# A scan feeding a mixture of experts: first tiles gathered a tile ahead, the padding row written later, and one conditional block put inside the other

## The chip, the cores and the metric

The kernel runs on one core of a Trainium2 chip. The metric is the device time of one execution in microseconds, as the median of several runs. One further execution is profiled, and all rows of a trace below come from that one.

## The reference

The input is a sequence of 4 x 5056 = 20224 tokens with 256 channels. A gated recurrence runs over the tokens of each of the four sequences, and its output is the input of a mixture of eight experts, of which each token uses one:

```
f = lower_bound + (1 - lower_bound) * sigmoid(f_logit)
h[t] = f[t] * h[t-1] + (1 - f[t]) * x[t]          # per sequence and channel
logits = h @ w_gate                               # 8 experts
e = argmax(logits); gate = softmax(logits)[e]; eom = sigmoid(h @ w_output_gate)[e]
out = gate * eom * (relu(h @ w1[e]) @ w2[e])      # w1: 256 x 1024, w2: 1024 x 256
```

## The kernel before

The kernel has two kinds of work that run interleaved.

**Chunks.** The tokens come in 40 chunks of 512 (`chunk`). For each chunk the SP queue loads the gate logits and the inputs, channels on the partitions (`load_chunk`, L250 and L251, two buffers each). ScalarE takes the tanh (L265), VectorE and ScalarE form the terms, VectorE runs the scan (L280). The result is scaled and split into a high and a low half in 16 bits (L310, L314), both halves lie in the buffer of the gate logits, and SP turns them into rows with DMA transposes (L307, four per chunk, into the tile `rows`). TensorE computes the router's logits (L329), VectorE picks the expert and the token's place among that expert's tokens, and POOL scatters each row, with a factor and the token's number behind it, to that place in a DRAM scratch `scr` (L433, an indirect DMA for each 128 tokens). A chunk is a generator that is cut into 17 steps; one "pump" advances every live chunk by one step, and a new chunk begins every eight pumps once the first ones are under way. In its fifth step a chunk asks for the next chunk's loads. The next but one chunk's loads use the same buffers, so they wait until the transposes have read them.

**Tiles.** A tile is a group of rows of one expert that is read back from `scr` by `gather`: SP reads the tile's address from a table that VectorE has filled (`plan_first`, `plan`), then issues a DMA transpose of the rows into `xq` (L630, three buffers) and a small load of their factors and token numbers into `mt` (L633, four buffers). Both wait for the scatters that the plan covers. The tile's factor `fac` on VectorE multiplies the factor in `mt` with a constant of the expert (L649). After two matrix products ScalarE scales the result by `fac` (L746), and POOL writes the rows to the output at the token numbers that it reads from `mt` (L750, an indirect DMA). An `mt` buffer is free again when that write is done.

The 16 *first tiles* (two rounds of one 128-row tile for each expert) run while the expert weights are still being loaded and split: `prep_load` loads half an expert's matrix in two pieces (L566), and other helpers scale and split it. Their work is cut by half tile. The loop over `j` from -2 to 15 (one half expert matrix each) calls `early` twice per `j`, then a drain loop calls it until all first tiles are through. Each call may gather one tile into `line`, takes the oldest tile of `line` one half further (`first1`, L715 to L717), makes the low half of the half before (`first_low`, L726), runs the second product of the half before that (`first2`, L735 to L737), and writes out finished tiles. A tile of expert `e` can be gathered when `j` is at least 2e+1 and computed from `j` = 2e+2. Between the calls `step` runs a number of pumps.

After that come the *later tiles*: 64 of 256 rows and a tail of up to 37 of 128 rows (`experts`). Each takes its expert's first matrix in a copy (L657), the products are L669 to L671 and L702 to L704. How many of the tail's 37 are used depends on the tokens. 18 of them are always run; the next 3 and the last 16 stand in two conditional blocks, one after the other, each behind a test of the count that every engine makes for itself (L964, L966). With these inputs neither block runs. Where a block is skipped, each engine brings the semaphores up to the values that the block would have left.

The order of the instructions: each engine works through its own queue in order. SP's queue follows the program's order. In the part up to the end of the first tiles (`prog["cut"]`) the scheduler of the framework may reorder the instructions of the four compute engines; behind that the order is as written. The first entries of SP's queue are a write of zero rows that stand for padding (`padt`, L211; POOL fills the tile, L209 and L210), then the loads of chunks 0 to 2 and the first weight pieces.

Of the kernel before, what the change touches and what calls it, by code (L numbers as in the profile page):

```python
# [45 lines left out]
def raw(ins):  # L46
    return getattr(ins, "ins", ins)
# [3 lines left out]
def tile_scan_moe(  # L51
# [10 lines left out]
    nc = tc.nc  # L62
    P = 128
# [10 lines left out]
    FREE = E * R  # L74
# [9 lines left out]
    def sure(tokens):  # L84

        return max(0, -(-(tokens - len(EARLY) * E * P - E * 255) // 256))
# [8 lines left out]
    scr = dp.tile([E * R + P, RW], I16, name="scr")  # L95
# [8 lines left out]
        out=tri, in_=ones, compare_op=ALU.is_gt, fill=0.0, base=0, pattern=[[1, P]], channel_multiplier=-1  # L104
# [63 lines left out]
    def alone(g):  # L168
# [12 lines left out]
        out=gsq, in0=wgf, scalar=1.0, in1=wgf, op0=ALU.mult, op1=ALU.mult, accum_out=gss  # L181
# [9 lines left out]
        out=wgs[:, :, 1, :], in0=wgc, scalar=gsc, in1=wgs[:, :, 0, :], op0=ALU.mult, op1=ALU.subtract  # L191
# [3 lines left out]
    fresh = []  # L195

    def apart(ins, group, keep=()):
        tc.declare_no_dep(raw(ins), group=group, keep=[raw(k) for k in keep], reason="rows apart")
        tc.add_to_no_dep_group(group, raw(ins))
# [8 lines left out]
    padt = cp.tile([P, RW], I16, name="padt")  # L208
    nc.gpsimd.memset(padt, 0)  # L209
    nc.gpsimd.iota(padt[:, CM + 2 : CM + 4].bitcast(I32), pattern=[[0, 1]], base=N, channel_multiplier=0)  # L210
    fresh.append(nc.sync.dma_start(out=scr[FREE : FREE + P, :], in_=padt))  # L211
    apart(fresh[0], "scr")
    row2 = [cp.tile([P, NB, RW], I16, name=f"rows{i}") for i in range(2)]

    top1 = w1f[:, (E - 1) * 2 * WH : E * 2 * WH]
# [344 lines left out]
    half = {}  # L560

    def prep_load(j):
        ws = []
        for i in range(2):
            w = wp.tile([P, QH], F32, tag="w", name="w")
            nc.sync.dma_start(out=w, in_=wT[j // 2][:, j % 2 * WH + i * QH : j % 2 * WH + (i + 1) * QH])  # L566
            ws.append(w)
        half[j] = dict(w=ws)
# [47 lines left out]
    def prep_lo(j, z):  # L616
        (h, r), (l, _) = parts(j, 0, z), parts(j, 1, z)
        yield BIG
        nc.vector.scalar_tensor_tensor(out=l, in0=r, scalar=half[j]["sc"], in1=h, op0=ALU.mult, op1=ALU.subtract)
# [4 lines left out]
    def gather(t, slot, e=None):  # L624
        tab, j, nb, new = slot
        n = nb * P
        r = nc.sync.value_load(tab[j : j + 1, 0:1], min_val=0, max_val=FREE + P - n)
        xq = gp.tile([P, 2, KD, 256], I16, tag="xq", name="xq")
        mt = gp.tile([P, 2, 4], I16, tag="mt", name="mt", bufs=4)
        i1 = nc.sync.dma_start_transpose(  # L630
            out=xq.rearrange("p a k n -> p (a k) n")[:, :, 0:n], in_=scr[ds(r, n), 0 : 2 * D]
        )
        i2 = nc.sync.dma_start(out=mt[:, 0:nb, :], in_=scr[ds(r, n), CM : CM + 4].rearrange("(b p) d -> p b d", p=P))  # L633
        for ins in (i1, i2):
            for k in new:
                tc.add_manual_dep(raw(ins), raw(k).name, DATA, reason="rows scattered")
            apart(ins, "scr", new)
        return dict(xh=xq[:, 0].bitcast(F16), xl=xq[:, 1].bitcast(F16), mt=mt, nb=nb, tab=tab, j=j, id=t, ev=e)
# [83 lines left out]
    def first_low(T, h):  # L722
        ph, hh = T[f"h{h}"]
        hl = ep.tile([P, 4, P], F16, tag="el", name="el", bufs=3)
        yield BIG
        nc.vector.scalar_tensor_tensor(out=hl, in0=ph, scalar=0.0, in1=hh, op0=ALU.max, op1=ALU.subtract)  # L726
        T[f"h{h}"] = (hh, hl)
# [31 lines left out]
    total = sure(N)  # L759
# [68 lines left out]
    line, pend, mid, over = [], [], [], []  # L828
    turns = [0] * len(EARLY)

    def early(j):

        if not line or line[0]["half"] == 1 and len(line) == 1:
            for r in range(len(firsts)):
                e = turns[r]
                if e < min(E, (j + 1) // 2) and (r == 0 or e < turns[r - 1]):
                    T = gather(f"f{r * E + e}", firsts[r][e], e)
                    T["half"] = 0
                    line.append(T)
                    turns[r] += 1  # L840
                    break
        tasks, wait, ready, late = [], list(pend), list(over), list(mid)
        pend.clear()
        over.clear()
        mid.clear()
        for T, h in wait:
            tasks.append(first_low(T, h))
            if h == 0:
                tasks.append(factors(T))
        go = line and line[0]["ev"] < j // 2  # L850

        def rest():
            for T in ready:
                evacuate(T)
                put(T)
            if go:
                T, h = line[0], line[0]["half"]
                T["half"] += 1
                if h == 1:
                    line.pop(0)  # L860
                first1(T, h)
                pend.append((T, h))
            for T, h in late:
                first2(T, h)
                if h == 1:
                    over.append(T)
            mid.extend(wait)

        return tasks, rest
# [6 lines left out]
            prep_load(n - 1)  # L876
    for n in range(min(EARLY[0], NCH) - 1, deep):
        prep_load(n)
    for j in range(-2, nh):
        tasks = []  # L880
        if 1 <= j < nh + 1 - deep:
            prep_load(j - 1 + deep)
        if 0 <= j + 1 < nh:
            tasks.append(prep_scale(j + 1))
        for z in range(2):
            if 0 <= j:
                tasks.append(prep_lo(j, z))
            mine, rest = early(j)
            tasks += mine
            step((PUMPS if j >= TURN else PUMPS0 if j >= 0 else FILL) / 2, tasks, LEAD)  # L890
            if 0 <= j + 1 < nh:
                prep_hi(j + 1, z)
            rest()
            tasks = []
            if j + 2 < nh:
                if z == 0:
                    prep_gram(j + 2)
                    tasks.append(prep_norm(j + 2))
                else:
                    prep_sum(j + 2)  # L900
# [10 lines left out]
    def ordered(start, cut):  # L911

        loose = [e.engine for e in (nc.vector, nc.scalar, nc.tensor, nc.gpsimd)]
        prev = {}
        for i, ins in enumerate(nc.cur_bb.bb.instructions[start:]):
            free = i < cut and ins.engine in loose
            if ins.engine in prev and not free:
                tc.add_manual_dep(ins, prev[ins.engine], AFTER, reason="order")
            prev[ins.engine] = ins.name

    def experts(t0, t1, more):
        ahead(t0)
        alone(expert(tiles[t0]))
        alone(fetch1(tiles[t0], 0))
        for t in range(t0, t1 + 2):
            T = tiles.get(t) if t < t1 else None
            U = tiles.get(t - 1) if t0 < t <= t1 else None
            V = tiles.get(t - 2) if t > t0 + 1 else None
            rate = RATE * (T or U or V)["nb"] / 2
            for q in range(4):  # L930
                tasks = []
                if q == 0:
                    if t + 1 < t1 + min(more, 1):
                        ahead(t + 1)
                    if T:
                        tasks.append(fetch1(T, 1))
                elif q == 2:
                    if t + 1 < t1:
                        alone(expert(tiles[t + 1]))
                        tasks.append(fetch1(tiles[t + 1], 0))  # L940
                elif q == 3 and T:
                    tasks.append(factors(T))
                if q == 0 and U:
                    tasks.append(low(U, 3))
                if q and T:
                    tasks.append(low(T, q - 1))
                step(rate, tasks)
                if q == 0 and V:
                    evacuate(V)
                if q == 1 and V:  # L950
                    put(V)
                if T:
                    gemm1(T, q)
                if U:
                    gemm2(U, q)

    cuts = [n for n in MORE if n < tail] + [tail]
    between["on"] = True
    experts(0, total + cuts[0], len(cuts) - 1)
    beside()  # L960
    ordered(0, prog["cut"])

    if len(cuts) > 1:
        used = nc.values_load(prog["count"][0:1, 0:1], min_val=0, max_val=tail)  # L964
        for a, b in zip(cuts[:-1], cuts[1:]):
            with tc.If(used > a):  # L966
                experts(total + a, total + b, 0)
                ordered(0, 0)


# [36 lines left out]
```

## Time and profile before

| what | us |
|---|---|
| runs | 986.54, 992.43, 989.42 |
| median of the runs | 989.42 |
| the profiled execution | 990.77 |
| its span, first to last instruction | 989.1 |
| TensorE busy, matmuls | 907.7 (92%) |
| VectorE busy | 801.0 (81%) |
| ScalarE busy | 519.7 (53%) |
| POOL busy | 390.1 (39%) |

The mean granted TensorE clock was 0.988. The busy times are averages over stages of different kinds, so they are read by stretches of the span. A wait in the profile names the instruction that waits and the one whose end released it. In a row of the timeline the first number is the start in microseconds, the second the duration, the bracket the idle time of the engine just before it and what ended that. Rows of SP with the letter q are instructions of its DMA queue.

### The profile page before, as it was taken

To read this page: it belongs to the slowest core of one execution; us is meant where nothing else is said; L and a number is where in the kernel's file an instruction comes from. 1 tells how busy PE (TensorE), PEld (TensorE's weight loads), DVE (VectorE), ACT (ScalarE), POOL (GpSimd) and SP (SyncE) were. 2 spreads that over 40 slices of the span, in tenths; PEclk is the share of its full clock that TensorE was granted. 3 is DMA by queue.
4 is the path that set the end of the run, shared out by engine and by line. 5 is a ranking of instruction groups with operands and counts; after the bars stand their busy time and mean duration, and the time that the engine had idled before them with its cause. 6 is when DMAs were issued, how large, how long until landed. Compare 5 with 4: busy or idle time off the path is not lost. (4 is left out here: it accounts for less than half of the span.)

```text
span 989.1 us, 30907 instructions
## 1 busy us (share of the span) xinstructions
PE 907.7 (92%) x9775; PEld 819.7 (83%) x9775; DVE 801.0 (81%) x2639; ACT 519.7 (53%) x1075; POOL 390.1 (39%) x378
## 2 busy tenths in 40 slices
PE   2258898899999999999999999999999999999993
PEld 2247887788888888888888888888888888899992
DVE  7989897888989988888898888888888886545550
ACT  6667675555555555555565555555555543333331
POOL 1432334434445454454545434455444443211111
PEclk9999999999999999999999999999999999999997
DMA  8899984855575657556576665655666544312120
GB/s 310 206 275 293 237 230 126 188 157 151 131 157 144 151 153 167 141 133 152 150 153 150 169 138 140 153 148 157 150 163 134 129 100 90 100 45 43 41 57 17
DMA packets 238558, 146.56 MB, mean 148 GB/s; under 512 B 202557, under 2 KB 204223, under 8 KB 238400
## 3 DMA queue, kind: packets, MB, share of 16 engines
q1 hardware_dynamic: 222752, 101.74, 44.9%
q0 software_dynamic: 15360, 42.74, 14.4%
q8 instruction: 95, 1.56, 0.7%
q14 instruction: 63, 0.52, 0.2%
q10 hardware_dynamic: 288, 0.02, 0.0%
HBM read 58.38 MB, written 44.49 MB: 104 GB/s over the span
## 5 line engine op out<-in xcount | busy, mean ns | idle before, releaser
L674 ACT ACTIVATE hh<-ph 128x512 f16<-128x512 f32 (+1 forms) x328 | 180.4, 550 | 307.8 <-PE ph L671 297.4
L669 PE MATMUL ph<-xq,w 128*128 128x256 f16 (+1 forms) x1312 | 330.4, 260 | 2.9 <-DMA xq<-scr 2.4
L671 PE MATMUL ph<-xq,w 128*128 128x256 f16 (+1 forms) x1312 | 331.1, 261 | 0.0
L670 PE MATMUL ph<-xq,w 128*128 128x256 f16 (+1 forms) x1312 | 330.9, 261 | 0.0
L750 POOL DMA_INDIRECT out_dram<-yo,mt x146 | 175.3, 1201 | 363.2 <-ACT yo L746 339.9
L704 PE MATMUL py<-w2s,hl 128*128 x1168 | 318.5, 273 | 0.0
L703 PE MATMUL py<-w2s,hh 128*128 x1168 | 318.4, 273 | 0.0
L702 PE MATMUL py<-w2s,hh 128*128 x1168 | 318.1, 272 | 0.0
L682 DVE SCALAR_TENSOR_TENSOR hl<-ph,hh 128x512 f16<-128x512 f32 (+1 forms) x328 | 204.9, 625 | 58.2 <-ACT hh L674 55.8
L433 POOL DMA_INDIRECT scr<-rows,dst x154 | 175.7, 1141 | 122.6 <-issue 109.3
L657 DVE COPY w<-w1s 128x2048 f16 x164 | 120.3, 734 | 35.1 <-PE ph L671 33.3
L669 PEld LDWEIGHTS <-w 128*128 128x128 f16 x1312 | 127.9, 98 | 14.3 <-DVE fac L649 2.7
L671 PEld LDWEIGHTS <-w 128*128 128x128 f16 x1312 | 128.0, 98 | 11.9
L670 PEld LDWEIGHTS <-w 128*128 128x128 f16 x1312 | 127.9, 97 | 9.7
L704 PEld LDWEIGHTS <-hl 128*128 128x128 f16 x1168 | 114.1, 98 | 13.8
L702 PEld LDWEIGHTS <-hh 128*128 128x128 f16 x1168 | 114.0, 98 | 11.4
L703 PEld LDWEIGHTS <-hh 128*128 128x128 f16 x1168 | 113.9, 98 | 10.6
L280 DVE TENSOR_TENSOR_SCAN xt<-ft,xt 128x512 f32<-128x512 f32 (+4 forms) x78 | 90.8, 1172 | 0.0
L746 ACT ACTIVATE yo<-py,fac 128x256 f32<-128x256 f32 x146 | 61.8, 468 | 26.7 <-PE py L704 26.1
L314 DVE SCALAR_TENSOR_TENSOR ft<-xt,sa,ft 128x512 f16<-128x512 f32 (+1 forms) x76 | 56.2, 744 | 20.1 <-ACT ft L265 18.3
L329 PEld LDWEIGHTS <-ft 128*128 128x128 f16 x600 | 51.7, 99 | 15.1 <-ACT ft L310 4.9
L310 ACT ACTIVATE ft<-xt,sa 128x512 f16<-128x512 f32 (+1 forms) x76 | 50.2, 707 | 23.3 <-DVE li L299 16.0
(171 smaller groups left out, 1298.7 us busy)
## 6 DMA issues: line engine op xcount, KB each, us to landing
ft<-in_fT_dram SPq DMA_DIRECT2D x37, 512.0 KB
xt<-in_xT_dram SPq DMA_DIRECT2D x37, 512.0 KB
w<-in_wT_dram SPq DMA_DIRECT2D x32, 512.0 KB
scr<-rows,dst POOLq DMA_INDIRECT x154
rows<-ft SPq DMA_TRANSPOSE x152
out_dram<-yo,mt POOLq DMA_INDIRECT x146
xq<-scr SPq DMA_TRANSPOSE x99
scr<-padt SPq DMA_DIRECT2D x9, 136.0 KB
```

The lines of the kernel that those rows point to most:

```text
L280: nc.vector.tensor_tensor_scan(out=xt[:, k, a:z], data0=ft[:, k, a:z], data1=xt[:, k, a:z], initial=init, op0=ALU.mult, op1=ALU.add)
L433: ins = nc.gpsimd.indirect_dma_start(out=scr[:, :], out_offset=IOA(ap=dst[:, b : b + 1], axis=0), in_=rows[:, b, :], in_offset=None)
L657: nc.vector.tensor_copy(out=w, in_=w1f[:, ds(T["ev"] * (2 * WH) + h * 2 * QH, 2 * QH)])
L669: nc.tensor.matmul(out=o, lhsT=w[:, f, k, 0, :], rhs=T["xh"][:, k, 0:n], start=first, stop=False)
L670: nc.tensor.matmul(out=o, lhsT=w[:, f, k, 0, :], rhs=T["xl"][:, k, 0:n], start=False, stop=False)
L671: nc.tensor.matmul(out=o, lhsT=w[:, f, k, 1, :], rhs=T["xh"][:, k, 0:n], start=False, stop=last)
L674: nc.scalar.activation(hh[:, :, 0:n], ph[:, :, 0:n], AF.Relu)
L682: nc.vector.scalar_tensor_tensor(out=hl[:, :, 0:n], in0=ph[:, :, 0:n], scalar=0.0, in1=hh[:, :, 0:n], op0=ALU.max, op1=ALU.subtract)
L702: nc.tensor.matmul(out=o, lhsT=hh[:, i, c], rhs=wh, start=first, stop=False, skip_group_check=True)
L703: nc.tensor.matmul(out=o, lhsT=hh[:, i, c], rhs=wl, start=False, stop=False, skip_group_check=True)
L704: nc.tensor.matmul(out=o, lhsT=hl[:, i, c], rhs=wh, start=False, stop=last, skip_group_check=True)
L750: ins = nc.gpsimd.indirect_dma_start(out=out[:, :], out_offset=IOA(ap=T["mt"][:, b, 2:4].bitcast(I32), axis=0), in_=T["yo"][:, b, :], in_o ...
```

## The change

Four edits. The write of the padding rows moves behind the loads of the prologue. `early` gathers a tile whenever fewer than two are in line. The factors of a first tile are made in the call after its second half, no longer in the call after its first. And the second conditional block stands inside the first, so that one test is made where the first block is skipped; with it the first later tile of a block is gathered inside the block.

```diff
     padt = cp.tile([P, RW], I16, name="padt")
     nc.gpsimd.memset(padt, 0)
     nc.gpsimd.iota(padt[:, CM + 2 : CM + 4].bitcast(I32), pattern=[[0, 1]], base=N, channel_multiplier=0)
-    fresh.append(nc.sync.dma_start(out=scr[FREE : FREE + P, :], in_=padt))
-    apart(fresh[0], "scr")
...
     def early(j):
 
-        if not line or line[0]["half"] == 1 and len(line) == 1:
+        if len(line) < 2:
             for r in range(len(firsts)):
...
         for T, h in wait:
             tasks.append(first_low(T, h))
-            if h == 0:
+            if h == 1:
                 tasks.append(factors(T))
...
     for n in range(min(EARLY[0], NCH) - 1, deep):
         prep_load(n)
+    fresh.append(nc.sync.dma_start(out=scr[FREE : FREE + P, :], in_=padt))
+    apart(fresh[0], "scr")
     for j in range(-2, nh):
...
-    experts(0, total + cuts[0], len(cuts) - 1)
+    experts(0, total + cuts[0], 0)
     beside()
     ordered(0, prog["cut"])
 
+    def rest_of(i):
+        if i + 1 < len(cuts):
+            with tc.If(used > cuts[i]):
+                experts(total + cuts[i], total + cuts[i + 1], 0)
+                ordered(0, 0)
+                rest_of(i + 1)
+
     if len(cuts) > 1:
         used = nc.values_load(prog["count"][0:1, 0:1], min_val=0, max_val=tail)
-        for a, b in zip(cuts[:-1], cuts[1:]):
-            with tc.If(used > a):
-                experts(total + a, total + b, 0)
-                ordered(0, 0)
+        rest_of(0)
```

## The prediction

> **What bounds the kernel now.** I read the page first, then the stretches table, the waits, and the timeline of the stretches that the change touches. The stretches table, cut at the points where the 16 first tiles end and where the last matmul ends (columns: busy time of PE, PEld, DVE, ACT, POOL, then granted clock, DMA share, GB/s):
>
> ```profile
> 0.00:184.00 184.00, 121.93 (x1652) 111.45 (x1652) 154.87 (x548) 119.32 (x216) 60.07 (x78) 0.98 0.89 235
> 184.00:973.00 789.00, 785.80 (x8124) 708.24 (x8123) 646.08 (x2092) 400.14 (x859) 329.07 (x299) 1.00 0.55 131
> 973.00:989.10 16.10, 0.00 (x0) 0.00 (x0) 0.00 (x0) 0.28 (x1) 0.98 (x1) 0.56 0.04 7
> ```
>
> There are three stages. In the middle one TensorE is busy 785.8 of 789.0 us, its matmuls and their order are not touched by the diff, so nothing is to be had there. The change can act on the first 184 us, where no engine is full (DVE 84%, PE 66%, DMA share 0.89) and the time is set by waits, and on the 16 us after the last matmul. Of the first stage's waits two belong to the gathers of first tiles, the weight side of TensorE left out:
>
> ```profile
> PE ph L715 <- DMA xq<-scr: 12.8, 6, 3.7
> DVE fac L649 <- DMA mt<-scr: 8.5, 7, 3.8
> ```
>
> (total us, times, longest.) Not all of the 12.8 us can be reached, as the call order below shows.
>
> **Part 1: the padding row written later.** The start, from the timeline and the SP queue's own waits:
>
> ```profile
> SPq L211 <- POOL rows L398: 2.7, 1, 2.7
> 0.83 0.38 ACTq L122 DMA_DIRECT2D lbt<-in_lbT_dram  x1
> ...
> 3.16 0.38 SPq L211 DMA_DIRECT2D scr<-padt  x1
> ...
> 3.60 0.42 SPq L250 DMA_DIRECT2D w2s<-in_fT_dram  x1
> ...
> 5.13 0.25 DVE L190 SCALAR_TENSOR_TENSOR wgs<-wgc,gts,wgs 128x32 f16<-128x32 f32 x1
> ...
> 7.65 1.15 ACT L265 ACTIVATE w2s<-w2s 128x512 f32<-128x512 f32 x2 [4.65 <-DMA w2s<-in_fT_dram]
> ...
> 9.04 1.29 DVE L269 SCALAR_TENSOR_TENSOR w2s<-w2s 128x512 f32<-128x512 f32 x2 [3.66 <-DMA w2s<-in_xT_dram]
> ```
>
> The first instruction of SP's queue is the padding write, which waits 2.7 us for POOL to fill its tile, and the first load stands behind it at 3.60. Without it that load can go when ACT's first one went, at 0.83: 2.8 us earlier, with all loads of the prologue behind it. ACT waits 4.65 and DVE 3.66 us for exactly these two loads, and DVE's own preparations end at 5.4, before the 6.3 that its next step would move to. So nothing else takes the wait's place and the shift is whole: 2.8 us. The write itself (0.38 us of SP) moves behind the last early weight load, where SP then waits for ACT anyway: nothing. Bounds: 2.3, if DVE's preparations or the shared start of the queues cost half a microsecond, and 3.2, if the write had also held the engines of the DMA.
>
> **Part 2: first tiles a tile ahead.** One call of `early` is one half tile. Before, tile n+1 is gathered in the call of tile n's second half; now in the call of its first half, where the expert's bound allows it. Following the loops with their counts of pumps (6 per half of j before j=0, then 1.5, then 1.125), the first four gathers stay where they are: rounds and experts are not ready sooner. From the fifth on each moves up by one call, but on SP's queue only five pass anything: the fifth passes the two loads of chunk 7, the seventh the first two row transposes of chunk 6, the eighth the other two, the fourteenth the first two of chunk 8, the fifteenth the other two. The rest stand in the same place of the queue as before.
>
> Now the middle of the stage:
>
> ```profile
> 92.81 0.38 SPq L250 DMA_DIRECT2D ft<-in_fT_dram  x1
> ...
> 99.12 1.15 ACT L265 ACTIVATE ft<-ft 128x512 f32<-128x512 f32 x2 [1.19 <-DMA ft<-in_fT_dram]
> 100.91 1.13 POOL L750 DMA_INDIRECT out_dram<-ey,mt  x1 [14.27 <-ACT ey L746]
> 101.01 0.23 PE L715 MATMUL ph<-xq,w1s 128*128 128x128 f16 x1 [2.00 <-DMA xq<-scr]
> 101.27 2.59 SPq L307 DMA_TRANSPOSE rows<-ft  x2
> 104.90 1.74 SPq L630 DMA_TRANSPOSE xq<-scr  x1
> 109.08 0.38 SPq L633 DMA_DIRECT2D mt<-scr  x1
> ...
> 113.01 2.59 SPq L307 DMA_TRANSPOSE rows<-ft  x2
> ...
> 119.45 0.38 SPq L250 DMA_DIRECT2D ft<-in_fT_dram  x1
> ...
> 121.78 0.22 PE L715 MATMUL ph<-xq,w1s 128*128 128x128 f16 x1 [1.05 <-DMA xq<-scr]
> 123.98 1.15 ACT L265 ACTIVATE ft<-ft 128x512 f32<-128x512 f32 x2 [3.57 <-DMA ft<-in_fT_dram]
> ```
>
> The fifth tile (PE idle 2.00 before 101.01) and the eighth (1.05 before 121.78) get their data sooner: 3.1 us of PE's waits. With the factors moved one call back, DVE loses all 8.5 us of its waits for `mt`, of which 3.8 lie at the fourteenth tile (below) and 4.7 here. Against that stands what is queued behind. A gather takes about 2.0 us of SP (161.89 to 163.88 below), so chunk 7's load goes 2.0 later than 92.81, and ACT, which already waited 1.19 for it, waits 3.2. The seventh gather is worse: `mt` has four buffers, so its load may only go when the third tile's output write (issued 100.91) has landed. In this trace SP stood at that point until 109.08. Passing the transposes of 101.27, SP reaches it at about 103.5 (the 2.0 us of a gather after 101.3) and stands there 5.6 us with the transposes behind it: they go at 109.5 instead of 101.3, those of 113.01 at about 115.5, behind the eighth gather, and the load of 119.45, which follows their landing, at about 122, 2.5 late. ACT waited 3.57 for that load. So gains of up to 4.7 on DVE face losses of up to 2.0 + 2.5 = 4.5 on ACT. I take a gain of 1.0, since DVE is the fuller engine; ends: +4.7 and -4.5.
>
> The Trainium skill, "DMA: Bandwidth & Descriptors" (section "Anatomy of one DMA"), speaks against the change here: it says that a DMA's semaphore fires only when its last byte is confirmed as landed, and that waits on semaphores are made by the issuing sequencer before dispatch, so an early gather holds its whole queue; the 8.2 us from 100.91 to 109.08 agree. By its fit of about 2.0 us plus bytes over 436 GB/s that write would, as an estimate, land near 103, and the hold would nearly vanish; the row decides.
>
> The end of the stage:
>
> ```profile
> 158.05 2.99 SPq L307 DMA_TRANSPOSE rows<-ft  x2
> 161.60 0.18 DVE L369 TENSOR_REDUCE km<-key 128x4 f32<-128x32 f32 x1
> 161.89 1.24 SPq L630 DMA_TRANSPOSE xq<-scr  x1
> ...
> 163.88 2.52 SPq L307 DMA_TRANSPOSE rows<-ft  x2
> 164.74 0.23 PE L715 MATMUL ph<-xq,w1s 128*128 128x128 f16 x1 [3.26 <-DMA xq<-scr]
> 165.58 0.21 DVE L649 TENSOR_SCALAR fac<-mt,cinv 128x1 f32<-128x1 f32 x1 [3.79 <-DMA mt<-scr]
> ...
> 171.72 0.96 POOL L433 DMA_INDIRECT scr<-rows,dst  x1 [5.67 <-DVE pl_av L497]
> ...
> 178.69 1.26 SPq L630 DMA_TRANSPOSE xq<-scr  x1
> ...
> 184.55 0.28 PE L669 MATMUL ph<-xq,w 128*128 128x256 f16 x1 [0.47 <-DVE w L657]
> ```
>
> The fourteenth gather stands behind transposes that wait for chunk 8's lower halves (158.05). PE idles 3.26 us for its rows and DVE 3.79 for its `mt`, and behind DVE's stall hang chunk 8's positions, its scatter at 171.72, and the gather of the first later tile at 178.69. Passing those transposes, it goes while SP is idle. PE runs nearly without gaps from 164.74 to 184.55, so its end moves by up to 3.26. What is late next: the transposes at 163.88 do not go sooner, because the fifteenth gather now stands ahead of them, and their landing bounds the scatter. I take 2.5 of the 3.26; ends 0 and 3.8.
>
> **Part 3: the second block inside the first.** Neither block runs here (82 later tiles, no more). The unused gather of tile 82 goes; SP waits for nothing behind it: 0. The rows of both skipped blocks and of the closing:
>
> ```profile
> 973.55 0.98 POOL L750 DMA_INDIRECT out_dram<-yo,mt  x1 [2.08 <-ACTq L966]
> L966 PEldq COMPARE_BRANCH  x2: 3852/4162/4472, 972.9 to 977.1; - x2
> L966 POOLq COMPARE_BRANCH  x2: 45/45/45, 973.9 to 976.5; - x2
> L966 POOLq INC_SWDGE_SEM  x2: 2322/2328/2335, 974.2 to 977.0; - x2
> L1003 POOLq DRAIN  x3: 40/107/8885, 979.4 to 988.8; - x3
> L1003 PEldq DRAIN  x2: 8/8/8, 981.9 to 988.7; - x2
> ```
>
> PE's second branch costs 4.47 us, but PE is through at 981.9. POOL ends the program: two skips, each a branch and a 2.33 us semaphore step (974.2 and 977.0), then a drain of 8.9 us from 979.4 to 988.3. One skip less starts the drain up to 2.86 us sooner (977.0 less 974.2). But the one step that is left accounts for writes on all queues' semaphores, so it must wait for the last write, issued 973.55 to 974.53 and by the rows landed before 977.0; I put it at 976.0, which leaves 1.0 us. What holds the drain for 8.9 us no row says: if it is tied to the last write, 0 comes; if to the two steps, 1.0 + 8.9/2, about 5.4.
>
> By the Trainium skill, "Runtime: NRT & Kernel Launch" (section "Instruction fetch mechanics"), a taken branch out of the fetched window stalls for a fetch; PE's 3.85 and 4.47 us agree. If the end hung on PE, 4.8 would come instead of 1.0.
>
> **Sum.** 2.8 + 1.0 + 2.5 + 1.0 = 7.3 us. The profiled execution took 990.77 us (span 989.1 and 1.7 around it): 983.5. It lies 1.35 above the median of the runs, 989.42, so the median forecast is 982.1 us.
>
> **Rivals.**
> (a) The gain at the fourteenth tile is swallowed: the fifteenth gather delays the transposes, the scatter stays near 171.7 and the gather of 178.69 with it. For: the queue's order; against: the scatter follows DVE's late positions. 989.4 - 4.8 = 984.6.
> (b) The closing drain depends on the skipped steps, or the end hangs on PE's branch: 989.4 - 7.3 - 4.4 = 977.7. For: two steps, one long drain; against: PE ends 6 us before POOL.
> (c) Slower: SP's hold at the seventh gather goes through whole. The price is 5.6 plus 2.0 for chunk 7's load, and no gain in this stage: 989.4 - 2.8 - 1.0 + 7.6 = 993.2. It decides once chunk 8's load goes more than 3.8 us later, counted from the first load, than now. For: ACT waits for loads at 99 and 124; against: SP catches up behind the weight loads.
> (d) The first load does not go at 0.83 because something else holds SP: 984.9. Against: the only wait in its rows is the one for POOL.
>
> **How the numbers follow.** Forecast 0.50 (979 to 985.5, from the bounds of the parts without their extremes together), (a) 0.17, (b) 0.15, (c) 0.08, (d) 0.05, and 0.05 for an order of the engines' work in the first stage that the scheduler, free there, changes for the worse by some 5 us. Leaving out most of (c) and the far end of (b), the range is 976.5 to 988. Half a per cent, about what this kernel's runs can tell from no change, is 4.9 us: faster means below 984.5. Faster: 0.46 of the forecast's, 0.15 of (b), 0.08 of (a) and 0.02 of (d), 0.71. Slower, above 994.4: 0.04. Same: 0.25.
>
> **What would show it.** Right: the first load near 0.8 and ACT's first activation near 4.9; no wait of `fac` for `mt`; PE not idle at the fourteenth tile; the first matmul of a later tile about 6 us earlier, near 178; TensorE's middle stage as long as before; POOL's drain starting about 1 us closer to the last write. Wrong: SP's wait at the seventh `mt` with longer ACT waits at chunks 7 and 8; the start of later tiles still above 181; a drain shorter or longer than 8.9 us.

## The result and the profile after

The changed kernel takes 1003.75 us (median; 1000.63 to 1005.82), the kernel before, run beside it, 988.89. The ratio is 1.0145 with a 95% interval of 1.0104 to 1.0185: 14.9 us slower, where the prediction had 7.3 us faster. The profiled execution took 1005.82 us, its span is 1004.0.

The stretches of the changed kernel, cut just before the first matmul of a later tile and after the last matmul (columns as in the prediction):

```profile
0.00:200.70 200.70, 123.05 (x1652) 111.28 (x1653) 157.16 (x556) 119.72 (x219) 63.86 (x80) 0.89 0.81 215
200.70:988.70 788.00, 787.01 (x8123) 708.75 (x8122) 641.22 (x2083) 399.58 (x856) 326.84 (x297) 1.00 0.56 131
```

The middle stage is what it was (788.0 us, 789.0 before, TensorE full). The whole loss lies in the first stage, which ends near 201 instead of 184.5. TensorE and VectorE are busy for about as long as before in it (123 and 157 us); they wait more. Its start went as predicted (rows of the timeline; after the change, lines behind the old place of the padding write stand two lower):

```profile
0.82 0.46 SPq L248 DMA_DIRECT2D w2s<-in_fT_dram  x1
4.59 1.15 ACT L263 ACTIVATE w2s<-w2s 128x512 f32<-128x512 f32 x2 [1.55 <-DMA w2s<-in_fT_dram]
6.25 1.29 DVE L267 SCALAR_TENSOR_TENSOR w2s<-w2s 128x512 f32<-128x512 f32 x2 [2.11 <-DMA w2s<-in_xT_dram]
```

The first load goes at 0.82 (3.60 before), ScalarE starts at 4.59 (7.65) and VectorE's scan work at 6.25 (9.04): 2.8 to 3.1 us. By chunk 6's load (70.92, before 70.06) that lead is gone, and at the end of the stage there is a lag of 16.6. Here the seventh gather with what follows it, and the way to the first later tile:

```profile
105.39 1.22 SPq L628 DMA_TRANSPOSE xq<-scr  x1
...
111.20 0.37 SPq L631 DMA_DIRECT2D mt<-scr  x1
111.67 3.69 SPq L305 DMA_TRANSPOSE rows<-ft  x2
...
145.56 0.96 POOL L431 DMA_INDIRECT scr<-rows,dst  x1 [2.16 <-issue]
...
190.67 0.97 POOL L431 DMA_INDIRECT scr<-rows,dst  x1 [5.62 <-issue]
...
196.96 1.26 SPq L628 DMA_TRANSPOSE xq<-scr  x1
...
201.17 0.37 PE L667 MATMUL ph<-xq,w 128*128 128x256 f16 x1 [5.80 <-DMA xq<-scr]
```

Read it from the bottom. The first later tile starts at 201.17, 5.80 us after TensorE ran dry, because its gather went at 196.96 (178.69 before). The gather follows the scatter of chunk 8, at 190.67 (171.72 before). Chunk 6's scatter goes at 145.56; before it went at 132.84. So 12.7 of the 19 us were lost by chunk 6's scatter, nearly all of them behind its load, which goes 0.9 late; the lead of 2.8 was used up ahead of it. The waits of the first stage (total us, times, longest), after and then two of the kernel before that were not shown:

```profile
DVE fac L647 <- DMA mt<-scr: 19.6, 8, 4.2
ACT ft L263 <- DMA ft<-in_fT_dram: 17.9, 4, 7.6
SPq L631 <- DMA out_dram<-ey,mt: 15.3, 4, 6.3
```

```profile
SPq L633 <- DMA out_dram<-ey,mt: 4.4, 2, 2.2
ACT ft L265 <- DMA ft<-in_fT_dram: 8.0, 5, 3.6
```

VectorE's waits for `mt` did not vanish, they grew from 8.5 to 19.6 us, and ScalarE's for the loads of the gate logits from 8.0 to 17.9. SP stands four times, 15.3 us, at the load of `mt` until an output write has landed. At the other end of the program:

```profile
989.11 0.98 POOL L748 DMA_INDIRECT out_dram<-yo,mt  x1 [2.06 <-ACT yo L744]
L965 POOLq EVENT_SEMAPHORE  x4: 17/43/43, 989.6 to 991.9; - x4
L965 POOLq INC_SWDGE_SEM  x1: 2342/2342/2342, 992.0 to 992.0; - x1
L1007 POOLq DRAIN  x3: 40/107/8885, 994.3 to 1003.8; - x3
```

From the last write to the end of the span it takes 14.9 us (1004.0 less 989.11); before it took 15.55 (989.1 less 973.55). One semaphore step is left. It starts at 992.0, 2.9 us after the last write's issue (the two of the kernel before started 0.65 and 3.5 after it), behind semaphore tests that end at 991.9. The drain is as long as before, 8.885 us.

### The profile page after: what moved, and what is told of

It reads as the page before. It is cut to its first block, busy times and chain, and to the rows that moved or that the text cites. A ratio compares the mean times of both kernels' runs of the same rounds, so it can differ in the third digit from the quotient of the medians.

```text
span 1004.0 us, 30882 instructions
## 1 busy us (share of the span) xinstructions
PE 910.1 (91%) x9775; PEld 820.0 (82%) x9775; DVE 798.4 (80%) x2639; ACT 519.4 (52%) x1075; POOL 391.7 (39%) x378
## 4 chain that ended last, share of the span: by engine, by line
PE 69%; issue 11%; DMA 8%; DVE 5%; POOL 3%; SPq 1%; ACT 1%; POOLq 0%; DVEq 0%; ACTq 0%
PE ph L667 11%; PE ph L668 11%; PE ph L669 11%; PE py L700 11%; PE py L702 11%; PE py L701 11%; DMA scr<-rows,dst 2%; POOL out_dram L748 2%; POOL scr L431 1%; DMA xt<-in_xT_dram 1%; DVE xt L278 1%; DMA rows<-ft 1%; PE pr L327 1%; DMA mt<-scr 1%; DMA ft<-in_fT_dram 1%
## 5 line engine op out<-in xcount | busy, mean ns | idle before, releaser
L748 POOL DMA_INDIRECT out_dram<-yo,mt x146 | 171.0, 1171 | 361.3 <-ACT yo L744 339.6
L431 POOL DMA_INDIRECT scr<-rows,dst x154 | 182.3, 1184 | 134.8 <-issue 116.3
L655 DVE COPY w<-w1s 128x2048 f16 x164 | 118.0, 720 | 34.3 <-PE ph L669 32.8
L312 DVE SCALAR_TENSOR_TENSOR ft<-xt,sa,ft 128x512 f16<-128x512 f32 (+1 forms) x76 | 56.0, 742 | 19.6 <-ACT ft L263 18.3
```

The costliest lines, as they stand in the source:

```text
L431: ins = nc.gpsimd.indirect_dma_start(out=scr[:, :], out_offset=IOA(ap=dst[:, b : b + 1], axis=0), in_=rows[:, b, :], in_offset=None)
L655: nc.vector.tensor_copy(out=w, in_=w1f[:, ds(T["ev"] * (2 * WH) + h * 2 * QH, 2 * QH)])
L748: ins = nc.gpsimd.indirect_dma_start(out=out[:, :], out_offset=IOA(ap=T["mt"][:, b, 2:4].bitcast(I32), axis=0), in_=T["yo"][:, b, :], in_o ...
```

## The experiments

Two theories stood at the start. **H**, the holds: SP stands at the load of `mt` and everything queued behind it comes late (the third rival of the prediction). **O**, the order: the change makes the scheduler, which is free in the first stage, place the instructions of the four compute engines differently there, and worse. A difference below is that of the medians, against the kernel before in the same comparison. The comparisons were made on several chips; on two of them (e5 to e8, e9 to e12) the kernel before takes 1012 us instead of 990.

**One part alone, and the holds taken away.**

e1_pad moves only the padding write:

```diff
-    fresh.append(nc.sync.dma_start(out=scr[FREE : FREE + P, :], in_=padt))
-    apart(fresh[0], "scr")
...
     for n in range(min(EARLY[0], NCH) - 1, deep):
         prep_load(n)
+    fresh.append(nc.sync.dma_start(out=scr[FREE : FREE + P, :], in_=padt))
+    apart(fresh[0], "scr")
```

> The kernel before with one edit: the padding row's write moved behind the prologue's loads. Theory H (holds: in the changed kernel SP stands at the loads of mt until an output write has landed, 15.3 us in the first stage against 4.4 before, and that is what costs): nothing is held here beyond before, the first load goes 2.8 us sooner, so 2 to 3 us faster than before, about 986. Theory O (order: the earlier loads make the scheduler order the compute engines' work of the first stage worse, and that costs): slower than before by 8 us or more, about 997 to 1004. Signs: start of the first later tile's matmuls 182 under H, above 192 under O.

e2_gather only gathers earlier:

```diff
-        if not line or line[0]["half"] == 1 and len(line) == 1:
+        if len(line) < 2:
```

> The kernel before with one edit: a first tile is gathered whenever fewer than two are in line. H: the holds come with it, SP waits 10 us or more for output writes at mt, and the kernel is 8 to 18 us slower than before, 997 to 1007. O: the start is as before and the order changes little, so within 4 us of before.

e3_all_mt7 is the whole change and e4_before_mt7 the kernel before, both with this edit:

```diff
-        mt = gp.tile([P, 2, 4], I16, tag="mt", name="mt", bufs=4)
+        mt = gp.tile([P, 2, 4], I16, tag="mt", name="mt", bufs=7)
```

> The changed kernel with seven buffers for mt in place of four (three more of 16 bytes a partition). H: SP's waits for output writes fall from 15.3 us to under 3, and most of the loss comes back: 982 to 990. O: the waits go but the time stays at 998 or more. If half comes back, both hold.

> The kernel before with seven buffers for mt. H: its two holds of 2.2 us each go; one of them stood before the eighth tile, so 0 to 4 us faster, 985 to 989. O says nothing of it: within 2 us of before.

Measured, beside a kernel before of 990.65: e1_pad 1000.83, +10.2 (ratio 1.0102, 1.0072 to 1.0132); e2_gather 996.14, +5.5 (1.0049, 1.0031 to 1.0066); e3_all_mt7 997.62, +7.0 (1.0063, 1.004 to 1.0087); e4_before_mt7 992.27, +1.6 (1.0014, 0.9995 to 1.0032). The striking one is e1: an edit that gives 2.8 us at the start, and moves one transfer to where SP waits anyway, loses 10.2. It moves no gather, so H as the prediction had it can't explain it. In its trace SP nevertheless stands 11.8 us at the loads of `mt` (4.4 in the kernel before), so the holds can come from the order too. e2 fits neither theory: 5.5 is less than H's 8 to 18 and more than O's 4; the traces show that its engines get another order as well. Without the holds (e3, whose order differs a little from that of the whole change) the change still loses 7.0. So H is at most a part: 4.6 to 7.9 us, if e3 is set against the whole change's 11.6 (e14, below) and 14.9, both on other chips. e4, the buffers alone, brings nothing.

The edit of the factors changes nothing here. With the gathers early, every engine gets the same instructions in the same order with it and without it.

**The order held.** To tell O from the rest, the following kernels hold the four compute engines to a written order, up to the end of the first stage. The order is that in which another kernel's engines get them, as ranks in the order of creation; SP keeps the program's order (the table `PLACES` and its reader `places` are left out):

```diff
-    ordered(0, prog["cut"])
+    ordered(0, prog["cut"]); pinned(nc, tc, prog["cut"])
...
+def pinned(nc, tc, cut):
+    made = nc.cur_bb.bb.instructions
+    for name, text in PLACES.items():
+        engine = getattr(nc, name).engine
+        own = [ins for ins in made[:cut] if ins.engine == engine]
+        rest = [ins for ins in made[cut:] if ins.engine == engine]
+        first = places(text)
+        line = [own[k] for k in first] + own[len(first):] + rest[:1]
+        for a, b in zip(line[:-1], line[1:]):
+            tc.add_manual_dep(b, a.name, AFTER, reason="order")
```

e5_pad_old_order is e1 and e7_gather_old_order e2, each with the order of the kernel before; e6_before_pads_order is the kernel before with the order of e1; e8_all_old_order is the whole change (without the factors' edit, which changes nothing) with the order of the kernel before.

> Only the padding write is moved, as in e1_pad, but TensorE, VectorE, ScalarE and GpSimd are held to the order of instructions that the kernel before has on them (manual dependencies written after the scheduling of each engine; SP keeps the moved write). Theory O (the scheduler, seeing the loads 2.8 us earlier, orders the engines' work of the first stage worse): the loss goes and the earlier start stays, 984.5 to 988.5, first matmul of a later tile near 182. Rival T (the order does no harm; the earlier loads themselves bunch up transfers and lengthen SP's holds): it stays where e1_pad was, 998 to 1003, first later matmul near 196.

> The kernel before, padding write in its old place, with the four engines held to the order that the kernel with the moved padding write has (one small iota of GpSimd stands four places later). Theory O: the order alone carries the loss, without the 2.8 us that the early start gives back: 999 to 1005, first later matmul near 199. Rival T: the loads are as late as before, so the time stays at 987 to 991.

> Only the gathers move a call earlier, as in e2_gather, with the four engines held to the order of the kernel before. Theory H (SP stands at the load of mt until an output write has landed, with transposes and loads behind it): the loss of e2_gather is the queue's and stays, 993 to 997, SP's waits for out_dram near 10 us in the first stage. Rival O: the loss of e2_gather came from the order as well, and goes, 986 to 990.

> The whole change (padding write moved, gathers a call earlier, second block in the first; the factors' call left where it was), with the four engines held to the order of the kernel before. Theory O alone: 981 to 985, what the prediction had. O and H together: the order's loss goes, SP's holds stay: 988 to 993. T: 1000 to 1004.

Beside a kernel before of 1012.09: e5 1010.05, -2.0 (0.9979, 0.9948 to 1.0009); e6 1018.97, +6.9 (1.007, 1.0029 to 1.0111); e7 1013.45, +1.4 (1.003, 1.0002 to 1.0058); e8 1008.61, -3.5 (0.9967, 0.9943 to 0.9991). The expected times were written for a kernel before of 989, so the differences count. Order and edit come apart: the kernel before, given nothing but the other order, gets slower, and the moved write, kept in the old order, does not. T, that the earlier loads do it themselves, falls. The 6.9 of e6 is less than the 10 or more that was expected. e7 shows that with the old order the early gathers cost little, where e2, on another chip, lost 5.5. The whole change gains 3.5 in that order: less than the 7.3 predicted. And holds alone don't make the loss: SP stands 12.1 us at the loads of `mt` in e8, which gains, and 11.6 in e9 below, which loses (two chips, both with a kernel before of 1012 us).

**Which engine, and what the gathers are worth.** e9_whole_again is the whole change; e10_whole_old_dve holds VectorE alone; e11_pad_nest_old_order leaves the early gathers out; e12_whole_mt7_old_order is e8 with seven buffers of `mt`.

> The whole change once more, so that it stands beside the runs below on one chip. Theories O (the scheduler's order) and H (SP's holds) alike: about 14 us above the kernel before, as the first time.

> The whole change (the factors' call left where it was) with VectorE alone held to the order of the kernel before; the scheduler is free on the other engines. Theory O in the form that VectorE's order is what counts (in the traces it has 18 us of other work between the positions of chunk 5 and the routing of chunk 6, where the kernel before has 9.9): nearly all of the loss goes, 4 below to 1 above the kernel before. If the order of TensorE and ScalarE counts as much, only a part goes: 4 to 10 above. H alone: 10 to 14 above.

> Without the early gathers: padding write moved and second block in the first, with the four engines held to the order of the kernel before. O: the two gains that the prediction had there, 2.8 and 0.7 to 1.0, and nothing lost: 3 to 4 below the kernel before. It tells what the early gathers are worth beside the kernel with the whole change in that order, which was 3.5 below: less than that is left if they help, more if they cost.

> The whole change in the order of the kernel before, with seven buffers of mt in place of four, so that no load of mt waits for an output write. H: SP's holds cost the early gathers what they could bring, so without them it is 6 to 8 below the kernel before (3.5 below with the holds). If the holds cost nothing once the order is kept: 3 to 4 below.

Beside a kernel before of 1011.9: e9 1017.76, +5.9 (1.0055, 1.0029 to 1.0081); e10 1011.87, 0.0 (1.0003, 0.9976 to 1.0029); e11 1007.61, -4.3 (0.9956, 0.9928 to 0.9983); e12 1008.02, -3.9 (0.9967, 0.9937 to 0.9997). e9 missed its expectation: 5.9 instead of 14. With VectorE held (e10) the time is that of the kernel before. But e10 doesn't single VectorE out: its trace shows TensorE, ScalarE and GpSimd, which are free there, in another order than in e9. And in the executions that were profiled most of the delay is still there: the first matmul of a later tile comes at 195.72 in e10, 198.41 in e9 and 188.03 in e11. The early gathers bring nothing here. e12 lies 0.4 lower than e8 did, well within the intervals of both, so no cost of the holds shows here in the old order.

**Control and the price on one chip.** e13_before_pinned holds the kernel before to its own order, e14_whole_third is the whole change, e15_whole_old_order is e8 again, e16_whole_old_others holds TensorE, ScalarE and GpSimd and leaves VectorE to the scheduler.

> Control: the kernel before with the four engines held to the very order that they have in it. Both theories: the same time as the kernel before, within 2 us; what it shows otherwise is what the holding itself costs, and is to be taken off the runs with a held order. Its trace also gives the kernel before's first stage on this chip.

> The whole change again, to stand beside the two runs that follow on one chip: 6 to 15 us above the kernel before, the two values measured so far. If O is right in kind and only the chip scales it, the first matmul of a later tile comes later than in the control by the same amount as the whole time.

> The whole change with the four engines held to the order of the kernel before, beside the whole change in its own order on the same chip. O: 2 to 5 below the kernel before, so that the difference of the two is the order's whole price. If the 14 us of the first comparison had another source than the order (SP's holds above all), it stays over 5 above the kernel before on a chip where the whole change costs 14.

> The whole change with TensorE, ScalarE and GpSimd held to the order of the kernel before, and VectorE left to the scheduler: the counterpart of e10. If VectorE's order carries the loss by itself: as far above the kernel before as the whole change. If the four orders hang together (VectorE can't run far out of step with what the others hand it): most of the loss goes here too, 3 below to 3 above.

Beside a kernel before of 990.34: e13 991.11, +0.8 (1.0005, 0.999 to 1.0021): holding an order costs nothing that shows. e14 1001.93, +11.6 (1.0119, 1.0104 to 1.0135). e15 989.81, -0.5 (0.9998, 0.9986 to 1.0011), short of the 2 to 5 expected. e16 997.22, +6.9 (1.0069, 1.0056 to 1.0082). So on one chip the order costs 12.1 us (e14 less e15). VectorE free and the others held keeps 7.4 of these 12.1 (e16 less e15), which meets neither expectation of e16. It isn't VectorE's order of e14 that is measured there: in the stretch of the next table e16 has two of VectorE's corrections, as the old order has, not six. Which engine's order carries the price stays open.

A rival falls by these traces, that a lower granted clock makes the loss: over the first 200 us it was 0.89 in e13 and 0.88 in e15, which lose nothing, and 0.95 in e14, which loses 11.6.

Where it goes is seen in the traces of e13 and e14 (lines as in the kernel before). First the groups of VectorE's weight corrections (L619) and its total, between the positions of chunk 5 and the moment at which chunk 6's routing (`dl`) begins, e13:

```profile
104.20:113.50 9.30, 8.10 (x29) 1.00 0.85 159
L619 DVE SCALAR_TENSOR_TENSOR w2s<-w,ws,w2s 128x1024 f16<-128x1024 f32 x2 | 2.6, 1276 | 0.0
```

and e14:

```profile
104.50:126.60 22.10, 17.25 (x49) 0.91 0.82 193
L619 DVE SCALAR_TENSOR_TENSOR w2s<-w,ws,w2s 128x1024 f16<-128x1024 f32 x4 | 5.1, 1279 | 0.0
L619 DVE SCALAR_TENSOR_TENSOR w1s<-w,ws,w1s 128x1024 f16<-128x1024 f32 x2 | 2.6, 1280 | 0.2 <-DMA w<-in_wT_dram 0.2
```

VectorE has two corrections of 1.28 us there in the old order and six in the new, 49 instructions instead of 29. Now the path of chunks 6 and 8 from the logits (L341) over `dl` (L360) to the scatter (L433), timeline of e13:

```profile
111.89 0.37 ACT L341 ACTIVATE lgp<-pr,li 128x128 f32<-128x128 f32 x1 [1.03 <-PE pr L329]
113.51 0.18 DVE L360 TENSOR_TENSOR dl<-lgo,mx 128x32 f32<-128x32 f32 x1
...
130.29 1.10 POOL L433 DMA_INDIRECT scr<-rows,dst  x1 [0.30 <-issue]
...
158.08 0.37 ACT L341 ACTIVATE lgp<-pr,li 128x128 f32<-128x128 f32 x1 [0.57 <-PE pr L329]
170.65 0.96 POOL L433 DMA_INDIRECT scr<-rows,dst  x1 [6.57 <-DVE pl_av L497]
...
183.53 0.28 PE L669 MATMUL ph<-xq,w 128*128 128x256 f16 x1 [0.48 <-DVE xv L142]
```

and of e14:

```profile
116.90 0.35 ACT L341 ACTIVATE lgp<-pr,li 128x128 f32<-128x128 f32 x1
121.78 0.21 DVE L649 TENSOR_SCALAR fac<-mt,cinv 128x1 f32<-128x1 f32 x1 [4.51 <-DMA mt<-scr]
126.58 0.17 DVE L360 TENSOR_TENSOR dl<-lgo,mx 128x32 f32<-128x32 f32 x1
...
142.68 0.96 POOL L433 DMA_INDIRECT scr<-rows,dst  x1 [1.90 <-issue]
...
167.48 0.37 ACT L341 ACTIVATE lgp<-pr,li 128x128 f32<-128x128 f32 x1
186.39 0.96 POOL L433 DMA_INDIRECT scr<-rows,dst  x1 [5.61 <-issue]
...
196.51 0.37 PE L669 MATMUL ph<-xq,w 128*128 128x256 f16 x1 [4.37 <-DMA xq<-scr]
```

In the old order chunk 6 needs 18.4 us from logits to scatter (111.89 to 130.29), in the new one 25.8 (116.90 to 142.68); chunk 8 needs 12.6 and 18.9. VectorE does the same work in both, but in the new order the corrections, which are for weights needed later, stand ahead of the routing, on which the next gathers hang. And a hold of SP is passed on: `fac` waits 4.51 us for `mt` at 121.78 while chunk 6's logits, ready since 116.90, stand behind it in VectorE's queue. The order's price thus contains the longer holds that it makes (14.0 us of standing at `mt` in e14, 8.9 in e15). And this stretch is not the whole price: chunk 6's load goes at 70.31 in e14 and at 66.06 in e15, so 4.2 us are lost ahead of it, at places that are not shown here. The first later tile comes 13.0 us later (196.51 less 183.53), about the 11.6 of the whole time.

**Why only 0.5 is gained with the order kept.** e17_pad_nest_again is e11 and e18_whole_mt7_again is e12, on another chip.

> As e11 (no early gathers, order of the kernel before), where 4.3 us were gained. With the whole change in this order only 0.5 us were gained (e15), and its trace has SP standing 5.4 us at the seventh gather's load of mt, as the third rival of the prediction had it, and ScalarE waiting 8.7 us for chunk 8's load, 3.4 in the control. H in that place: the early gathers cost about 3 us, so 3 to 4.5 below the kernel before here. If the gathers cost nothing: 0 to 2 below.

> As e12 (whole change, order of the kernel before, seven buffers of mt), beside e17 on one chip. H: without the hold the early gathers bring what the prediction had for them, 3.5 us at the fourteenth tile and before it: 5 to 7 below the kernel before. If the fourteenth tile's gain is swallowed later (the first rival): as e17, 3 to 4.5 below.

Beside a kernel before of 990.25: e17 987.0, -3.3 (0.997, 0.9954 to 0.9987); e18 987.77, -2.5 (0.9984, 0.9971 to 0.9998). So padding write and blocks bring 3.3, the early gathers take 2.8 of it (e15), and about 0.8 if the holds are away (e18). e18 meets neither of its expectations: without holds the gathers bring no gain. e15 ran on another chip than e17 and e18, its interval touches that of e17 and overlaps that of e18, and on the chips with 1012 us the same step is 0.8 (e8 against e11). No comparison in the old order shows a gain of the early gathers; that they cost 2.8 us is likely, not certain. The timeline of e13, for the place of the seventh gather:

```profile
99.57 3.31 SPq L307 DMA_TRANSPOSE rows<-ft  x2
104.11 1.23 SPq L630 DMA_TRANSPOSE xq<-scr  x1
...
117.05 0.38 SPq L250 DMA_DIRECT2D ft<-in_fT_dram  x1
...
121.44 1.15 ACT L265 ACTIVATE ft<-ft 128x512 f32<-128x512 f32 x2 [3.40 <-DMA ft<-in_fT_dram]
...
163.07 0.23 PE L715 MATMUL ph<-xq,w1s 128*128 128x128 f16 x1 [3.56 <-DMA xq<-scr]
```

and of e15, the whole change in the same order:

```profile
97.49 1.24 POOL L750 DMA_INDIRECT out_dram<-ey,mt  x1 [14.96 <-ACT ey L746]
98.20 1.23 SPq L630 DMA_TRANSPOSE xq<-scr  x1
104.79 0.37 SPq L633 DMA_DIRECT2D mt<-scr  x1
105.26 3.67 SPq L307 DMA_TRANSPOSE rows<-ft  x2
...
119.99 0.38 SPq L250 DMA_DIRECT2D ft<-in_fT_dram  x1
...
124.10 1.15 ACT L265 ACTIVATE ft<-ft 128x512 f32<-128x512 f32 x2 [8.65 <-DMA ft<-in_fT_dram]
...
150.33 1.39 SPq L630 DMA_TRANSPOSE xq<-scr  x1
...
175.13 0.28 PE L735 MATMUL py<-w2s,eh 128*128 128x256 f16 x1 [4.10 <-ACT eh L719]
```

The seventh gather passes the transposes, and SP stands from 99.4 (98.20 and 1.23) to 104.79, 5.4 us. The transposes go at 105.26, 5.7 later than in the control, chunk 8's load 2.9 later, and ScalarE waits 8.65 instead of 3.40 us for it (6.35 in e17, which has no early gathers). The fourteenth gather goes at 150.33 and its wait on TensorE is gone, as predicted. But TensorE idles 4.10 us at 175.13, in the second product of the fifteenth tile, which waits for ScalarE; ScalarE had just stood 5.68 us for the load of chunk 10 (0.30 in the control). And chunk 8's scatter goes at 170.42, with 170.65 in the control.

The hold at `mt` is not all that delays chunk 8's load. The eighth gather stands ahead of the second pair of chunk 6's transposes now, and chunk 8's load waits until these have landed. Here e18, where nothing is held at `mt`, and then e17, where that gather follows the pair:

```profile
100.86 2.54 SPq L307 DMA_TRANSPOSE rows<-ft  x2
...
111.03 1.23 SPq L630 DMA_TRANSPOSE xq<-scr  x1
...
112.93 2.52 SPq L307 DMA_TRANSPOSE rows<-ft  x2
119.26 0.38 SPq L250 DMA_DIRECT2D ft<-in_fT_dram  x1
```

```profile
108.31 2.56 SPq L307 DMA_TRANSPOSE rows<-ft  x2
111.91 1.23 SPq L630 DMA_TRANSPOSE xq<-scr  x1
...
116.90 0.38 SPq L250 DMA_DIRECT2D ft<-in_fT_dram  x1
```

Without the hold the first pair goes 4.4 us sooner than in e15 (100.86, 105.26), but the second pair goes at 112.93 in both, and the load at 119.26 is only 0.7 sooner than in e15 and still 2.4 later than in e17. So more buffers of `mt` don't free that load.

Of these runs, the version without the early gathers and with the order held (e11, e17) beats both kernels: by 3.3 to 4.3 us against the one before.

## Why the prediction was wrong

**The step that failed** is the one on the scheduler: "0.05 for an order of the engines' work in the first stage that the scheduler, free there, changes for the worse by some 5 us". The mechanism was named and nearly dismissed. It came, and it cost 12.1 us (e14 less e15). The whole change cost 14.9 us in the first comparison, 11.6 in e14 and 5.9 in e9, on chips where the kernel before itself differs. Their engines get the same order in all three, so what makes them differ stays open; it is not the granted clock alone (0.89 over the first stage in the first profile, but 0.95 in e14 and 0.96 in e9). Nor did a run test why the scheduler chose this order, only that it did and what it costs.

**Part 1, padding write: right at its place, wrong as a term.** The shift of 2.8 is there (0.82, 4.59, 6.25), and in the old order it stays: e5 gains 2.0, and e17, with the tail's 0.7, 3.3. But "nothing else takes the wait's place" looked at the engines' data alone. Moving the write also changed the order that the scheduler wrote: alone, this edit costs 10.2 us (e1).

**Part 2, middle: the wrong end taken.** The prediction took +1.0 between +4.7 and -4.5. In e15 the hold came nearly to the number: 5.4 us standing (5.6 said), transposes 5.7 later (8.2 said), chunk 8's load 2.9 later (2.5 said). Counted from the first load, as rival (c) counts, the load is 5.7 late, past its point of 3.8; but the loss of 3.8 us that (c) ties to it didn't come in this order (-0.5 against the kernel before), and 2.6 of the 5.7 are there in e17 without an early gather. What didn't come either is the gain: the edit of the factors doesn't move `fac`, and VectorE's waits for `mt` went from 8.3 (e13) to 5.1 us in e15, not to none. The Trainium skill, "DMA: Bandwidth & Descriptors" (section "Anatomy of one DMA"), says that the waits are made by the issuing sequencer and that an issued transfer's semaphore fires on the landing; e15 agrees. Its fit would have the write of 97.49 land after 2.3 us (an estimate: 2.0 plus 128 KB over 436 GB/s). SP was released 7.3 us after that write's issue began, and the measured number decides.

**Part 2, fourteenth tile: taken 2.5, measured about nothing.** The wait of 3.56 went away in e15 and a wait of 4.10 came in the next tile. This is rival (a) in its result, though not by its way. `fac` no longer waits there (4.07 us in e13), but chunk 8's logits come at 159.86 instead of 158.08, after its late load, and the scatter stays. Early gathers together were put at +3.5; they measure -2.8 (e17 against e15; other chips, same order), and -0.8 without holds (e17 against e18, one chip).

**Part 3, tail: right.** 1.0 said, 0.65 measured by the rows. The step left over stood behind semaphore tests until 991.9, 1.8 us after the last write was issued, and the drain kept its 8.885 us. That rules out (b): the drain doesn't depend on the number of steps, and TensorE's branch isn't the end (its queue reaches the closing at 992.5, POOL's drain ends at 1003.2).

So the sum is 3.3 gained at the ends (e17), 2.8 lost by the gathers (e15 against e17) and 12.1 lost by the order (e14 against e15): +11.6, where -7.3 was said. Only the last term and the total are from one chip.

## What to carry to other kernels

Where a scheduler is free, an edit that moves an input can have a second effect, the order that is then written. Its price isn't bounded by the edit's own size (e1 shifted the start by 2.8 us and lost 10.2), so ask for both. One place to look is how much work that could wait stands on the same engine as a critical chain. To measure an edit, hold the old order and change the edit alone; to keep a gain, write the order down. And before a transfer is moved up in a queue, look at which buffer it needs, when the last reader of it lands, and what then stands behind it: here a queue that stood for 5 us and transposes that went late gave back what the move gained.

## What the chip showed that was not expected

- An indirect write of 128 rows held its buffer for about 7 us after its issue in e15's first stage (97.49 to 104.79).
- POOL's closing drain took 8.885 us after one skipped block as after two.
- On the chips of e5 to e12 the middle stage, which no edit touches, isn't full. From 300 to 500 us TensorE is busy 196.31 us in e11 and 200.00 in e13, both at the full granted clock. The matmuls of the later tiles last 272 ns in both. What TensorE waits for there no row names. So comparisons hold on one chip; across chips only the differences were used.
